# Attention scores as products of 64 rows, one head each, in the two halves of TensorE's rows

## The chip, the cores and the metric

The kernel runs on one core of a Trainium2 chip. The metric is device time in microseconds (us) of one execution. Before the change it is 565.6 us, the median of three runs (565.58 to 567.75). A profiled execution is somewhat longer, here 585.4 us; shares and single durations are read from it, the total is not.

In the notation of the profile, PE is TensorE's matmul row, PEld its weight loads, DVE is VectorE, ACT is ScalarE, POOL is GpSimd, and SP is SyncE, which issues most of the DMA transfers here. "L662" is line 662 of the kernel.

## The reference

Two blocks follow each other. The first is attention with a local window: 4 batches, 8 heads, 768 tokens, 64 elements a head. A chunk of 32 queries sees 8 memory keys and the keys from 16 before its start to 8 after its end. The second sends each token to the one of 8 experts with the highest gate, and scales the result by the gate.

```python
for c in range(nc):
    q_c = q[:, :, c_start:c_end]
    k_full = np.concatenate([mem_k, k[:, :, l_start:r_end]], axis=2)
    v_full = np.concatenate([mem_v, v[:, :, l_start:r_end]], axis=2)
    scores = scale * np.matmul(q_c, k_full.transpose(0, 1, 3, 2))
    a = softmax(scores)                      # written out in the reference
    out[:, :, c_start:c_end] = np.matmul(a, v_full)
x = out.transpose(0, 2, 1, 3).reshape(B * S, H * D)      # 3072 x 512
expert_idx = np.argmax(x @ w_gate, axis=1)
y[rows of e] = np.maximum(x[rows of e] @ w1[e], 0) @ w2[e]   # 512 -> 1024 -> 512
return gate_w[:, None] * y
```

## The kernel before

Everything is float32. The attention works on 32 blocks of 96 queries (QB = 96), and each block looks at a window of 128 keys. Queries and keys arrive by DMA for two blocks at a time, in token rows; TensorE transposes them, so that the 64 elements of a head lie on 64 partitions: even heads on partitions 0 to 63, odd heads on 64 to 127. Two heads thus share 128 partitions. The keys of such a pair stand as the weights of the array (128 rows by 128 keys). The queries stream through it, and each head's queries have zeros in the other head's half:

```python
qTs = [kpool.tile([128, H // 2, 2, 2, QB], F32, name=f"qT{i}") for i in range(NQ)]
for i, t in enumerate(qTs):
    nc.vector.memset(t[0:D, :, 1], 0.0)
    nc.gpsimd.memset(t[D:128, :, 0], 0.0)
...
def turn_heads(name, u, x):
    t = ps_t.tile([128, H // 2, QB], F32, tag="t", name="tqk")
    for a in range(H // 2):
        turn(t[:, a], units[u][name][:, 2 * a + x], ident[0:QB, 0:QB])
    return t

def turn_q(u, x):
    units[u]["qT"] = qTs[u % NQ]
    t = turn_heads("q", u, x)
    for j in range(2):
        (nc.vector.tensor_copy if x else nc.scalar.copy)(
            qTs[u % NQ][D * x : D * x + D, :, x, j], t[D * j : D * j + D]
        )
...
def scores(i):
    s, (b, qb) = st[i], divmod(i, NQB)
    w0 = window(qb)
    p0 = QB // 2 * (i % 2)
    sc = ps_s.tile([128, H, 128], F32, tag="s", name="sc")
    for a in range(H // 2):
        mm(
            sc[:, 2 * a : 2 * a + 2, 0:QB].rearrange("p x (j t) -> p x j t", j=2),
            lhsT=turned[b][:, a, w0 : w0 + WIN],
            rhs=units[i // 2]["qT"][:, a, :, :, p0 : p0 + QB // 2],
            start=True,
            stop=True,
        )
    ex = s["ex"] = apool.tile([128, H, QB], F32, name="ex")
    ...                                       # three exponentials over all heads, on ScalarE

def values(i, g, bank):
    ...
    for j in range(4):
        h = 4 * g + j
        mm(o[:, j], lhsT=s["ex"][:, h], rhs=s["v"][:, h], start=True, stop=True)
    ...                                       # VectorE divides by the sums and writes x
```

One turn of the attention's loop holds, in this order on TensorE, work of several blocks (cut; the rest of a turn is routing and DMA issues):

```python
for i in range(NB + 3):
    ...                                       # loads for later blocks
    if u < NU:
        f(u, 0)                               # half of the transposes of a later q or k
    need(i, scores)
    ...
    if 0 <= i - 1 < NB:
        values(i - 1, 0, banks[0])
    need(i - 2, turn_xb)                      # transposes of the result, for the gate
    late = logits(i - 3, banks[1]) if 0 <= i - 3 < NB else None
    if 0 <= i - 1 < NB:
        values(i - 1, 1, banks[1])
    ...
    if u < NU:
        f(u, 1)                               # the other half of the transposes
```

PSUM holds two `sc` tiles of two banks each, two tiles of transposes and two banks for `values` and `logits`. A block's keys window lies in `turned[b]`, with the memory keys between the keys of each block; they come there through four transposes of 32 rows at the start (`tm`, line 615). The experts follow the attention in the same program.

Of the kernel before, what the change touches and what calls it, by code (L numbers as in the profile page):

```python
# [10 lines left out]
F32 = mybir.dt.float32  # L11
# [8 lines left out]
B, H, S, D = 4, 8, 768, 64  # L20
NMEM = 8
CHUNK, LEFT, RIGHT = 32, 16, 8
QB = 96
# [41 lines left out]
WIN = 128  # L65
PER = QB + NMEM
KW = NQB * PER
NV, NQ = 6, 3
# [25 lines left out]
def window(qb):  # L94
    return min(max(PER * qb - LEFT, 0), KW - WIN)
# [415 lines left out]
def ordinary(ctx, tc, q, k, v, mem_k, mem_v, moe_w_gate, moe_w1, moe_w2, out, good):  # L511

    nc = tc.nc
    mm, turn = nc.tensor.matmul, nc.tensor.transpose

    def bc(ap, axis, n):
        shape = list(ap.shape)
        shape.insert(axis, n)
        idx = tuple([slice(None)] * axis + [None])
        return ap[idx].to_broadcast(shape)  # L520
# [6 lines left out]
    kpool = actx.enter_context(tc.tile_pool(name="kpool", bufs=1))  # L527
# [23 lines left out]
    wg = cpool.tile([128, DM // 128, E], F32, name="wg")  # L551
    nc.scalar.dma_start(wg, moe_w_gate.rearrange("(c p) e -> p c e", p=128))

    qTs = [kpool.tile([128, H // 2, 2, 2, QB], F32, name=f"qT{i}") for i in range(NQ)]
    for i, t in enumerate(qTs):
        nc.vector.memset(t[0:D, :, 1], 0.0)
        nc.gpsimd.memset(t[D:128, :, 0], 0.0)

    mk = kpool.tile([B * NMEM, H, D], F32, name="mk")
    for b in range(B):  # L560
# [35 lines left out]
    turned = {}  # L596

    units = [dict() for _ in range(NU)]
# [20 lines left out]
# [10 lines that stand above are left out]
        t = turn_heads("q", u, x)  # L629
        for j in range(2):  # L630
            (nc.vector.tensor_copy if x else nc.scalar.copy)(
                qTs[u % NQ][D * x : D * x + D, :, x, j], t[D * j : D * j + D]
            )

    def place_mem(b):
# [20 lines left out]
    def scores(i):  # L656
        s, (b, qb) = st[i], divmod(i, NQB)
        w0 = window(qb)
        p0 = QB // 2 * (i % 2)
        sc = ps_s.tile([128, H, 128], F32, tag="s", name="sc")  # L660
        for a in range(H // 2):
            mm(  # L662
                sc[:, 2 * a : 2 * a + 2, 0:QB].rearrange("p x (j t) -> p x j t", j=2),
                lhsT=turned[b][:, a, w0 : w0 + WIN],
                rhs=units[i // 2]["qT"][:, a, :, :, p0 : p0 + QB // 2],
                start=True,
                stop=True,
            )
        ex = s["ex"] = apool.tile([128, H, QB], F32, name="ex")
        x = 0 if qb == 0 else 2 if qb == NQB - 1 else 1  # L670
        sc4 = sc[:, :, 0:QB].rearrange("p h (j t) -> p h j t", j=2)
        ex4 = ex.rearrange("p h (j t) -> p h j t", j=2)
        for g in range(3):
            sl = slice(CHUNK // 2 * g, CHUNK // 2 * g + CHUNK // 2)
            nc.scalar.activation(  # L675
                ex4[:, :, :, sl], sc4[:, :, :, sl], AF.Exp, bias=mask[:, 3 * x + g : 3 * x + g + 1], scale=D**-0.5
            )

    def values(i, g, bank):
        s = st[i]  # L680
        if g == 0:
            s["x"] = xr[:, i % NXR, 0:DM]
        o = bank[0:QB, 0 : 4 * (D + 1)].rearrange("p (h d) -> p h d", h=4)
        for j in range(4):
            h = 4 * g + j
            mm(o[:, j], lhsT=s["ex"][:, h], rhs=s["v"][:, h], start=True, stop=True)  # L686

        inv = inv_all[:, i, 4 * g : 4 * g + 4]
        nc.vector.reciprocal(inv, o[:, :, D])  # L689
        x = s["x"].rearrange("p (h d) -> p h d", h=H)  # L690
        nc.vector.tensor_tensor(x[:, 4 * g : 4 * g + 4], o[:, :, 0:D], bc(inv, 2, D), op=OP.mult)
# [162 lines left out]
    with tc.manual_schedule():  # L854
# [8 lines left out]
        for name, u in ((turn_k, 0), (turn_q, 0), (turn_k, 1)):  # L863
            name(u, 0)
            name(u, 1)
            if name is turn_q:
                turn_mem()
                place_mem(0)
        for i in range(NB + 3):

            u = i // 2 + 1 + i % 2
            which, f = ("q", turn_q) if i % 2 == 0 else ("k", turn_k)
            if i % 2 == 0 and u + 2 < NU:
                load_unit("k", k, u + 2)
# [3 lines left out]
            if u < NU:  # L878
                f(u, 0)
            need(i, scores)  # L880
            banks = [ps_o.tile([128, 512], F32, tag="o", name="o") for _ in range(2)]
            then = []
# [5 lines left out]
            if 0 <= i - 1 < NB:  # L888
                values(i - 1, 0, banks[0])
# [3 lines left out]
            if 0 <= i - 1 < NB:  # L893
                values(i - 1, 1, banks[1])
# [16 lines left out]
            for g in range(last):  # L911
                t = GROUPS[g][0] + i - GROUPS[g][1] - 4
# [28 lines left out]
    h = mpool.tile([128, KH, 2, HALF], F32, name="h")  # L941
# [341 lines left out]
@with_exitstack  # L1283
def kernel(ctx, tc, *args):
    nc = tc.nc
    gpool = ctx.enter_context(tc.tile_pool(name="gpool", bufs=1))
    good = gpool.tile([1, 1], I32, name="good")
    rv = ordinary(tc, *args, good)
    with tc.If(rv == 0):
        general(tc, *args)  # L1290
# [28 lines left out]
```

## Time and profile before

| part of the span | us | what TensorE does there |
|---|---|---|
| 0 to 14.6 | 14.6 | waits for the first loads, first transposes |
| 14.6 to about 160 | 145.4 | the 32 blocks; matmul row busy 139.7 us, weight loads 137.7 us |
| 160 to 220 | 60.0 | routing, last scatters, a first short run of experts; matmul row busy 55.5 us |
| 220 to 570 | 350.0 | the experts; matmul row busy 334.0 us |

A matmul's duration in the profile runs from its start to its modelled end, and matmuls follow each other before that end. So durations add up to more than the time, and what one costs is the distance between starts. A float32 matmul shows as two records, each with a weight load; a float32 transpose shows as one. In the groups of part 5, the shape is weights (rows*columns) followed by the streamed columns, then the count, the busy time and the mean duration in ns, and last the idle time of the engine just before, with what ended it.

The profile's granted TensorE clock is 1.00 for most of the attention stage and 0.5 in its first microseconds.

### The profile page before, as it was taken

What the parts mean: (1) busy time and instruction counts of PE and PEld (TensorE: products, weight loads), DVE (VectorE), ACT (ScalarE), POOL (GpSimd) and SP (SyncE); (2) the same over time, 40 slices, a digit from 0 to 9 for tenths busy, and PEclk for the clock granted to TensorE, in tenths of its full rate; (3) what the DMA queues carried; (4) which work ended last, traced back from release to release, by engine and by line L of the source; (5) the groups of instructions that cost most, each with busy time, mean ns of one, the idle gap of its engine ahead of it and who ended that gap; (6) DMA issues with size and microseconds to landing.
All of it is one profiled execution on the core that took longest, in us unless ns stands there. A gap on an engine that the chain in (4) does not pass through costs nothing. (4 is left out here: it accounts for less than half of the span.)

```text
span 585.4 us, 10593 instructions
## 1 busy us (share of the span) xinstructions
PE 534.9 (91%) x3850; PEld 503.9 (86%) x3850; DVE 323.7 (55%) x757; ACT 175.8 (30%) x414; POOL 133.9 (23%) x174
## 2 busy tenths in 40 slices
PE   3999899999999899988999999979999999999950
PEld 3999899999978489988899999969999999988850
DVE  4556555656536519539378368356393874929220
ACT  3556455645412113023231132122232402232010
POOL 3500212313154630050240043230201503010020
PEclk9999999999959999988999999998999999999985
DMA  9999999999132256082252184230232807200010
GB/s 173 187 170 203 229 192 231 210 214 219 31 94 83 74 169 225 13 284 99 91 200 78 34 294 119 85 142 1 67 125 97 308 8 251 94 19 10 0 47 32
DMA packets 81655, 76.13 MB, mean 130 GB/s; under 512 B 39852, under 2 KB 64556, under 8 KB 81456
## 3 DMA queue, kind: packets, MB, share of 16 engines
q1 hardware_dynamic: 72368, 54.54, 39.8%
q0 software_dynamic: 8128, 19.29, 9.8%
q14 instruction: 147, 1.20, 0.7%
q8 instruction: 52, 0.85, 0.6%
q10 hardware_dynamic: 960, 0.24, 0.2%
HBM read 65.04 MB, written 16.45 MB: 139 GB/s over the span
## 5 line engine op out<-in xcount | busy, mean ns | idle before, releaser
L1023 POOL DMA_INDIRECT out_dram<-y,tg x36 | 39.0, 1084 | 135.3 <-ACT y L1017 115.6
L1113 ACT ACTIVATE h<-h 128x288 f32<-128x288 f32 (+6 forms) x72 | 33.7, 476 | 110.9 <-DVE h L1142 53.3
L1086 PE MATMUL b<-xT,w 128*128 128x256 f32 (+1 forms) x288 | 60.7, 369 | 0.0
L1086 PEld LDWEIGHTS b<-xT,w 128*128 128x128 f32 x288 | 52.3, 190 | 6.7 <-issue 0.5
L686 PE MATMUL o<-v,ex 128*96 128x65 f32 x512 | 55.6, 253 | 1.0 <-PE o L686 1.0
L686 PEld LDWEIGHTS o<-v,ex 128*96 128x96 f32 x512 | 52.2, 169 | 1.1 <-issue 1.1
L662 PE MATMUL sc<-qT,kT 128*128 128x192 f32 x256 | 50.4, 342 | 0.0
L675 ACT ACTIVATE ex<-sc,cst 128x256 f32<-128x256 f32 x96 | 38.4, 470 | 30.7 <-PE sc L662 27.4
L1086 PE MATMUL b<-h,w 128*128 128x144 f32 (+6 forms) x288 | 46.6, 317 | 0.0
L825 POOL DMA_INDIRECT xe<-x_dram,rows x38 | 40.8, 1074 | 25.0 <-PE b L1086 10.8
L1086 PE MATMUL b<-xS,w 128*128 128x144 f32 (+6 forms) x288 | 46.4, 311 | 0.0
L1086 PEld LDWEIGHTS b<-h,w 128*128 128x128 f32 x288 | 43.7, 201 | 0.8
L1086 PE MATMUL b<-xS,wT 128*128 128x144 f32 (+6 forms) x288 | 44.4, 307 | 0.0
L1086 PE MATMUL b<-big,w 128*128 128x144 f32 (+6 forms) x288 | 44.4, 307 | 0.0
L662 PEld LDWEIGHTS sc<-qT,kT 128*128 128x128 f32 x256 | 43.1, 199 | 0.0
L1086 PE MATMUL b<-big,wT 128*128 128x144 f32 (+6 forms) x288 | 42.9, 307 | 0.0
L1124 ACT COPY big<-b 128x288 f32<-128x288 f32 (+6 forms) x18 | 7.6, 425 | 117.2 <-PE b L1086 102.7
L1086 PEld LDWEIGHTS b<-xS,w 128*128 128x128 f32 x288 | 42.1, 194 | 0.8
L689 DVE RECIPROCAL inv_all<-o 96x4 f32<-96x4 f32 x64 | 11.4, 178 | 55.9 <-PE o L686 47.5
L1086 PEld LDWEIGHTS b<-xS,wT 128*128 128x128 f32 x288 | 41.2, 190 | 1.1 <-issue 0.3
L1086 PEld LDWEIGHTS b<-big,w 128*128 128x128 f32 x288 | 41.4, 190 | 0.8
L1086 PEld LDWEIGHTS b<-big,wT 128*128 128x128 f32 x288 | 41.0, 190 | 0.8
(150 smaller groups left out, 863.6 us busy)
## 6 DMA issues: line engine op xcount, KB each, us to landing
w<-in_moe_w_dram SPq DMA_DIRECT2D x64, 512.0 KB
kn<-in_k_dram SPq DMA_DIRECT2D x16, 384.0 KB
qn<-in_q_dram SPq DMA_DIRECT2D x16, 384.0 KB
v<-in_v_dram SPq DMA_DIRECT2D x24, 128.0 KB
v<-in_v_dram SPq DMA_DIRECT2D x24, 112.0 KB
v<-in_v_dram SPq DMA_DIRECT2D x8, 144.0 KB
v<-in_v_dram SPq DMA_DIRECT2D x8, 96.0 KB
xe<-x_dram,rows POOLq DMA_INDIRECT x38
```

The costliest lines, as they stand in the source:

```text
L662: mm(sc[:, 2 * a : 2 * a + 2, 0:QB].rearrange("p x (j t) -> p x j t", j=2), lhsT=turned[b][:, a, w0 : w0 + WIN], rhs=units[i // 2]["qT"][: ...
L675: nc.scalar.activation(ex4[:, :, :, sl], sc4[:, :, :, sl], AF.Exp, bias=mask[:, 3 * x + g : 3 * x + g + 1], scale=D**-0.5)
L686: mm(o[:, j], lhsT=s["ex"][:, h], rhs=s["v"][:, h], start=True, stop=True)
L689: nc.vector.reciprocal(inv, o[:, :, D])
L825: nc.gpsimd.indirect_dma_start(out=to.bitcast(I32), out_offset=None, in_=x_dram, in_offset=bass.IndirectOffsetOnAxis(ap=which, axis=0), bo ...
L1023: i = nc.gpsimd.indirect_dma_start(out=out, out_offset=bass.IndirectOffsetOnAxis(ap=token.bitcast(I32), axis=0), in_=y, in_offset=None, bo ...
L1086: mm(bank[:, q, 0:hf], lhsT=w[i][:, c, 128 * (q0 + q) : 128 * (q0 + q) + 128], rhs=a[i][:, c], start=c == 0, stop=c == k - 1,)
L1113: relu = lambda o: nc.scalar.activation(o, o, AF.Relu)
L1124: nc.scalar.copy(T(p), P(1, p))
```

## The change

Each head becomes a product of its own. Its weights are its keys alone (64 rows by 128 keys), and its 96 queries stream through these 64 rows. Even heads use rows 0 to 63 of the array and odd heads rows 64 to 127, and the code takes them in turn. The zero halves of the query tile are no longer needed, nor are the six memsets that wrote them. The scores of the even heads go to one bank of PSUM and those of the odd heads to the other, so the order of heads in `sc` and `ex` becomes even heads first, and `values` reads its weights from there. The aim is to stop streaming columns against zeros and to let the two row halves of the array work side by side.

```diff
--- before.py
+++ after.py
@@ -551,10 +551,7 @@
     wg = cpool.tile([128, DM // 128, E], F32, name="wg")
     nc.scalar.dma_start(wg, moe_w_gate.rearrange("(c p) e -> p c e", p=128))
 
-    qTs = [kpool.tile([128, H // 2, 2, 2, QB], F32, name=f"qT{i}") for i in range(NQ)]
-    for i, t in enumerate(qTs):
-        nc.vector.memset(t[0:D, :, 1], 0.0)
-        nc.gpsimd.memset(t[D:128, :, 0], 0.0)
+    qTs = [kpool.tile([128, H // 2, 2, QB], F32, name=f"qT{i}") for i in range(NQ)]
 
     mk = kpool.tile([B * NMEM, H, D], F32, name="mk")
     for b in range(B):
@@ -629,7 +626,7 @@
         t = turn_heads("q", u, x)
         for j in range(2):
             (nc.vector.tensor_copy if x else nc.scalar.copy)(
-                qTs[u % NQ][D * x : D * x + D, :, x, j], t[D * j : D * j + D]
+                qTs[u % NQ][D * x : D * x + D, :, j], t[D * j : D * j + D]
             )
 
     def place_mem(b):
@@ -657,15 +654,18 @@
         s, (b, qb) = st[i], divmod(i, NQB)
         w0 = window(qb)
         p0 = QB // 2 * (i % 2)
+
         sc = ps_s.tile([128, H, 128], F32, tag="s", name="sc")
         for a in range(H // 2):
-            mm(
-                sc[:, 2 * a : 2 * a + 2, 0:QB].rearrange("p x (j t) -> p x j t", j=2),
-                lhsT=turned[b][:, a, w0 : w0 + WIN],
-                rhs=units[i // 2]["qT"][:, a, :, :, p0 : p0 + QB // 2],
-                start=True,
-                stop=True,
-            )
+            for x in range(2):
+                half = slice(D * x, D * x + D)
+                mm(
+                    sc[:, H // 2 * x + a, 0:QB].rearrange("p (j t) -> p j t", j=2),
+                    lhsT=turned[b][half, a, w0 : w0 + WIN],
+                    rhs=units[i // 2]["qT"][half, a, :, p0 : p0 + QB // 2],
+                    start=True,
+                    stop=True,
+                )
         ex = s["ex"] = apool.tile([128, H, QB], F32, name="ex")
         x = 0 if qb == 0 else 2 if qb == NQB - 1 else 1
         sc4 = sc[:, :, 0:QB].rearrange("p h (j t) -> p h j t", j=2)
@@ -683,7 +683,7 @@
         o = bank[0:QB, 0 : 4 * (D + 1)].rearrange("p (h d) -> p h d", h=4)
         for j in range(4):
             h = 4 * g + j
-            mm(o[:, j], lhsT=s["ex"][:, h], rhs=s["v"][:, h], start=True, stop=True)
+            mm(o[:, j], lhsT=s["ex"][:, H // 2 * (h % 2) + h // 2], rhs=s["v"][:, h], start=True, stop=True)
 
         inv = inv_all[:, i, 4 * g : 4 * g + 4]
         nc.vector.reciprocal(inv, o[:, :, D])
```

## The prediction

> **What bounds the kernel now.** I read the page first, then the order of matmuls in one block of the attention stage, then the waits of the queue that issues the loads. The first two lines of the page's part 1 show TensorE's two rows busy nearly all the time; the three groups of part 5 are the line that changes and one that feeds from it.
>
> ```profile
> PE 534.9 (91%) x3850; PEld 503.9 (86%) x3850; DVE 323.7 (55%) x757; ACT 175.8 (30%) x414; POOL 133.9 (23%) x174
> ...
> L662 PE MATMUL sc<-qT,kT 128*128 128x192 f32 x256 | 50.4, 342 | 0.0
> L675 ACT ACTIVATE ex<-sc,cst 128x256 f32<-128x256 f32 x96 | 38.4, 470 | 30.7 <-PE sc L662 27.4
> ...
> L662 PEld LDWEIGHTS sc<-qT,kT 128*128 128x128 f32 x256 | 43.1, 199 | 0.0
> ```
>
> The scores are 32 blocks x 4 matmuls = 128 instructions, but 256 records: each float32 product is a weight load and a matmul, twice. Neither row was idle before them (0.0), while ScalarE waited 27.4 us for them. The durations 342 and 199 ns overlap, so what a product costs has to be read from the start times. One block of the steady part, from the timeline of TensorE alone (start, duration, line, count):
>
> ```profile
> 29.68 1.49 PE L662 MATMUL sc<-qT,kT 128*128 128x192 f32 x8
> 31.01 0.81 PE L686 MATMUL o<-v,ex 128*96 128x65 f32 x8
> 31.66 0.50 PE L696 MATMUL tx<-cst,big 96*128 96x96 f32 x4
> 32.00 0.77 PE L710 MATMUL o<-wg,xT 128*96 128x8 f32 x8
> 32.62 0.87 PE L686 MATMUL o<-v,ex 128*96 128x65 f32 x8
> 33.33 0.50 PE L623 MATMUL tqk<-cst,qn 96*128 96x96 f32 x4
> 33.67 0.49 PE L623 MATMUL tqk<-cst,kn 96*128 96x96 f32 x4
> 34.00 1.49 PE L662 MATMUL sc<-qT,kT 128*128 128x192 f32 x8
> ```
>
> From 29.68 to 34.00 is 4.32 us a block without a hole, so the stage is bound by TensorE. The scores hold it from 29.68 to 31.01: 1.33 us for 8 records, 166 ns each. All their time is on the path; 32 blocks make 42.6 us, the most that could be won here.
>
> Is it the stream or the weight load that sets 166 ns? Four more groups of the timeline, from the experts, give the rule:
>
> ```profile
> 506.85 1.95 PE L1086 MATMUL b<-big,w 128*128 128x96 f32 x16
> 508.63 1.95 PE L1086 MATMUL b<-h,w 128*128 128x96 f32 x16
> ...
> 239.63 2.12 PE L1086 MATMUL b<-big,w 128*128 128x144 f32 x16
> 241.59 3.62 PE L1086 MATMUL b<-xT,w 128*128 128x256 f32 x16
> ```
>
> 144 columns: (241.59 - 239.63) / 16 = 122 ns. 256 columns: the last of the 16 starts about 3.24 us after the first (3.62 less the 0.379 us of one record), so 216 ns. That is 0.84 ns a column and a constant of about 2 ns: the stream sets it, and 192 columns make 163 ns, as the scores show. But 96 columns should then take 82 ns and take (508.63 - 506.85) / 16 = 111 ns. So a new set of 128 weight columns has a floor of about 112 ns. The changed products have 96 columns each and lie on that floor.
>
> [...] The kernel has one place that bears on the last: four transposes of 32 rows between transposes of 96 rows, at the half clock of the start. No trace of it bears on the overlap. [...]
>
> ```profile
> 11.12 0.60 PE L615 MATMUL tm<-cst,mk 32*128 32x32 f32 x4 [1.51 <-DMA mk<-in_mem_k_dram]
> 11.65 0.90 PE L623 MATMUL tqk<-cst,kn 96*128 96x96 f32 x4
> ```
>
> One record of the first kind lasts 0.289 us, so the last of the four starts at 11.72 - 0.289 = 11.43; the next kind starts at 11.65, 0.22 us later, where its fellows follow at 0.10. Its own second record is late too: a record lasts 0.37 us there, so the fourth starts at 11.65 + 0.90 - 0.37 = 12.18, so three gaps take 0.53 instead of 3 x 0.16 = 0.48. Together about 0.17 us for one switch, at half clock. If the part in the array halves at full clock and the part of the weight load doesn't, a switch costs 0.08 to 0.17 us. This is an estimate from one place.
>
> **The change part by part.**
> 1. Six memsets of the zero halves go: three of 0.70 us on VectorE, three of 0.73 us on GpSimd, all over by 3.5 us, while the first transpose waits for its data until 5.82. Worth 0.
> 2. The copies that fill qT keep their size (64x384, 474 and 556 ns), the exponentials theirs (128x256, 470 ns). The order of heads is only a matter of addresses. Worth 0.
> 3. Four products of 192 columns (8 records) become eight of 96 (16 records), in pairs over the two row halves. Half of the columns that streamed before met zeros, so the columns per head halve; the weight loads double in number, each of 64 rows by 128 columns.
>    - If loads and streams of the two halves run side by side, each half has 8 records at 112 ns: 8 x 112 = 0.90 us against 1.33, a gain of 0.43 us a block.
>    - If the loads go one after another: 16 x 112 = 1.79 us, a loss of 0.46 us a block.
> 4. Before and after the scores stand products of 96 and 128 rows. So there are two switches a block, 0.17 to 0.33 us together.
>
> The sum with side-by-side loads: 0.90 + 0.25 = 1.15 against 1.33, 0.18 us a block, 5.8 us over 32 blocks (3.2 to 8.3 with the span of the switches). One after another: 1.79 + 0.25 - 1.33 = 0.71 us, 23 us more.
>
> **Does the gain reach the end?** The loads might not follow. In 14.6 to 144 us the DMA engines show a share of over 1 and 187 to 217 GB/s, so I read what the issuing queue waits for there:
>
> ```profile
> SPq L603 <- PE tqk L623: 7.0, 9, 2.4
> SPq L603 <- PE sc L662: 4.1, 3, 2.3
> SPq L603 <- PE o L686: 2.6, 4, 1.9
> SPq L603 <- PE tx L696: 2.5, 2, 2.1
> SPq L610 <- PE o L686: 1.9, 1, 1.9
> ```
>
> It waits 18 us of 129 for TensorE to release buffers, about 14%. A block shorter by 0.2 us (5%), even by 0.43 (10%), is still fed. VectorE and ScalarE are busy for 85 and 80 of the 145 us of the stage. Behind the attention the experts begin when the last block is counted and sent, so a shorter stage moves them forward whole.
>
> **The rivals.** (a) Loads serialize: for it, the weight floor of 111 ns shows the load path is already a limit, and each product is two passes of the same row half in sequence, not alternating halves. [...] It gives 565.6 + 23 = 588. (b) Everything overlaps and switches are nearly free: 32 x 0.43 = 13.8 us less, 552. Against it, the 0.17 us seen after the transposes of 32 rows. (c) The loads by DMA become the bound: the time stays within 3 us of before. Its share of over 1 speaks for it, the 14% of waits against it. (d) The switches cost more than estimated[...]: 0.45 us a block would eat the gain and leave 566.
>
> **Range and chances.** I give the side-by-side loads 0.6, less certain because two passes stand in each half. With them the time lies between 552 and 566, most likely at 565.6 - 5 = 561; 2% is 11.3 us, so only rival (b) or nearly that is faster by over 2%: a third of the 0.6. Without them (0.4) it is mostly 580 to 591, beyond 2%, unless loads overlap in part. So 0.20 faster, 0.47 within 2%, 0.33 slower; the range 552 to 590 has to hold both branches, and the middle between them is the least likely.
>
> **What would show it.** In the changed profile: 512 records on the line of the scores, and the time from the first of them to the next group per block, near 1.15 us (loads overlap), 0.9 (switches free) or over 1.9 (loads serial). Start times of pairs a few ns apart would show the overlap; a hole between the last transpose and the first score the switch. The other groups of the block should keep their lengths, and new waits of the transposes for kn or qn would be the DMA. I am wrong if the time leaves 552 to 590, or if the block is shorter but the attention stage ends no earlier.

## The result and the profile after

The changed kernel takes 671.1 us, the median of four runs (669.75 to 672.66), against 565.8 us for the kernel before (four runs, 565.58 to 567.75). The ratio is 1.185, with a 95% interval of 1.182 to 1.189. That is 105 us more, far outside the predicted range of 552 to 590. Ratios, here and below, leave out runs over 1.5% above the fastest of their kernel.

The page of the profile after, part 1 and the granted clock of part 2 (40 slices, tenths), and from part 5 the values (line 686), the scores (line 662) and the exponentials (line 675):

```profile
PE 631.6 (95%) x4106; PEld 591.1 (88%) x4106; DVE 321.8 (48%) x754; ACT 178.4 (27%) x414; POOL 131.3 (20%) x171
...
PEclk9999999999999999999999999999999999999995
...
L686 PE MATMUL o<-v,ex 128*96 128x65 f32 x512 | 97.5, 369 | 0.9 <-PE o L686 0.9
L686 PEld LDWEIGHTS o<-v,ex 128*96 128x96 f32 x512 | 88.2, 278 | 5.5 <-issue 4.2
...
L662 PE MATMUL sc<-qT,kT 64*128 64x96 f32 x512 | 64.8, 431 | 0.0
L675 ACT ACTIVATE ex<-sc,cst 128x256 f32<-128x256 f32 x96 | 38.5, 471 | 71.1 <-PE sc L662 71.0
```

TensorE is busier than before, not waiting more. But the values of line 686, whose size and number the change leaves alone (only the head that they read from `ex` is found elsewhere), went from a mean of 253 ns to 369. ScalarE's exponential is where it was, 471 ns against 470. One block in the timeline of TensorE (start, duration, what) shows it better:

```profile
38.53 2.02 PE L662 MATMUL sc<-qT,kT 64*128 64x96 f32 x16
40.48 1.54 PE L686 MATMUL o<-v,ex 128*96 128x65 f32 x8
41.82 0.84 PE L696 MATMUL tx<-cst,big 96*128 96x96 f32 x4
42.46 1.34 PE L710 MATMUL o<-wg,xT 128*96 128x8 f32 x8
43.65 1.52 PE L686 MATMUL o<-v,ex 128*96 128x65 f32 x8
44.97 0.84 PE L620 MATMUL tqk<-cst,qn 96*128 96x96 f32 x4
45.61 0.84 PE L620 MATMUL tqk<-cst,kn 96*128 96x96 f32 x4
46.38 2.03 PE L662 MATMUL sc<-qT,kT 64*128 64x96 f32 x16
```

From 38.53 to 46.38 a block takes 7.85 us against 4.32 before. Every group but the scores has about doubled: line 710 from 0.62 us (32.00 to 32.62) to 1.19, the two groups of transposes from 0.67 us to 1.41, with their switch (the change between products over different numbers of rows). Only the scores grew less, from 1.33 to 1.95 us. By these start distances TensorE runs at half clock through the whole attention, and its matmul row is busy for all of it (237.4 of the 237.4 us from 14.6 to 252.0). The first and the last scores start at 14.7 and 252.0 us, 237.3 us apart; before they were 142.2 us apart. Before's profiled run was itself 20 us longer than its timed runs, so it is a poor measure here. Against the control with fillers below (135.1 us), the attention lost 102 us, which is the whole 105 but for 3.

The clock row of the page says 9 in these slices. It can't be believed: the trace's own clock records begin with their first change, which is the opening at 274.3 us, and the row fills the time ahead of it with full clock. The start distances agree with the record and not with the row: equal products of the experts follow each other at 427 ns up to 273.97 us and at 216 ns from 274.36 us on. The same filling hid the half clock of the first 17.5 us before, where transposes follow each other at 160 ns (12.02 to 12.82 us) and only from 17.54 us on at 83: the profile shows 1.00 there, so my sentence on the clock ahead of the prediction, that it grants 0.5 in the first microseconds, is wrong as a reading of the profile. The half clock follows from the start times alone. That sentence also leaves out that before's clock closed for 3.4 us at 72.1 us, inside the attention, with 0.5 in its record. The distance between starts is the evidence: 0.16 us a transpose in (0.84 - 0.36) / 3, against 0.08 in the fast kernel.

The pairs do run side by side. Four single records of the scores, start in us and row half by the order of the code:

```
38.529  even head, first pass
38.536  odd head
38.851  even head
38.857  odd head
```

The two of a pair start 6 to 7 ns apart. The second pair comes 0.32 us after the first; the six behind it follow at 213 ns each, nearly twice the 112 ns that I had given them.

### The profile page after: what moved, and what is told of

It reads as the page before. It is cut to its first block, busy times and chain, and to the rows that moved or that the text cites. A ratio compares the mean times of both kernels' runs of the same rounds, so it can differ in the third digit from the quotient of the medians.

```text
span 668.0 us, 11099 instructions
## 1 busy us (share of the span) xinstructions
PE 631.6 (95%) x4106; PEld 591.1 (88%) x4106; DVE 321.8 (48%) x754; ACT 178.4 (27%) x414; POOL 131.3 (20%) x171
## 5 line engine op out<-in xcount | busy, mean ns | idle before, releaser
L686 PE MATMUL o<-v,ex 128*96 128x65 f32 x512 | 97.5, 369 | 0.9 <-PE o L686 0.9
L686 PEld LDWEIGHTS o<-v,ex 128*96 128x96 f32 x512 | 88.2, 278 | 5.5 <-issue 4.2
L662 PE MATMUL sc<-qT,kT 64*128 64x96 f32 x512 | 64.8, 431 | 0.0
L662 PEld LDWEIGHTS sc<-qT,kT 64*128 64x128 f32 x512 | 57.1, 324 | 7.0 <-issue 6.7
L710 PEld LDWEIGHTS o<-wg,xT 128*96 128x96 f32 x256 | 44.7, 280 | 0.0
L1086 PE MATMUL b<-h,w 128*128 128x144 f32 (+6 forms) x288 | 44.3, 307 | 0.0
L710 PE MATMUL o<-wg,xT 128*96 128x8 f32 x256 | 42.7, 297 | 0.0
L773 POOL DMA_INDIRECT x_dram<-big,dest x32 | 29.7, 927 | 64.0 <-DVE dest L765 38.2
L1086 PEld LDWEIGHTS b<-h,w 128*128 128x128 f32 x288 | 41.3, 190 | 0.8
```

The lines of the kernel that those rows point to most:

```text
L662: mm(sc[:, H // 2 * x + a, 0:QB].rearrange("p (j t) -> p j t", j=2), lhsT=turned[b][half, a, w0 : w0 + WIN], rhs=units[i // 2]["qT"][half, ...
L686: mm(o[:, j], lhsT=s["ex"][:, H // 2 * (h % 2) + h // 2], rhs=s["v"][:, h], start=True, stop=True)
L710: mm(ps, lhsT=s["xT"][:, c], rhs=wg[:, c], start=c == 0, stop=c == DM // 128 - 1)
L773: i = nc.gpsimd.indirect_dma_start(out=x_dram, out_offset=bass.IndirectOffsetOnAxis(ap=dest[:, t : t + 1], axis=0), in_=xr[:, t % NXR].bit ...
L1086: mm(bank[:, q, 0:hf], lhsT=w[i][:, c, 128 * (q0 + q) : 128 * (q0 + q) + 128], rhs=a[i][:, c], start=c == 0, stop=c == k - 1,)
```

## The experiments

Theory A, a guess of mine: with half the columns streamed, the attention is too sparse for the clock to open, and nothing before the experts opens it. Rivals: A2, it is the 64-row products or their switches, not the missing columns; B, the clock is only lost at the start, and once open it stays; C, something other than the clock slows TensorE.

Each of the first four kernels ran once, on one chip, where the kernel before took 567.1 us.

**The burst at the start.** Eight full matmuls ahead of the loop, in the changed kernel:

```diff
+        warm = ps_s.tile([128, H, 128], F32, tag="s", name="sc")
+        for _ in range(8):
+            mm(warm[:, 0:4], lhsT=ones, rhs=bc(ones, 1, 4), start=True, stop=True)
         for i in range(NB + 3):
```

> The changed kernel with eight matmuls of 128 rows by 512 columns ahead of the first block (16 records, about 10 us of added work), so that TensorE enters the attention at full clock. Theory A, the changed block is too sparse to keep the clock: [...] starts of paired scores are 213 ns apart again and the time is about 671 + 8 = 679 us. Theory B, only the warm start was lost and a warm TensorE stays warm: [...] a block of about 4.15 us, and a time near 561 + 8 = 569 us.

Measured: 571.2 us. A block deep in the attention, from the timeline of TensorE:

```profile
101.71 1.14 PE L662 MATMUL sc<-qT,kT 64*128 64x96 f32 x16
102.78 0.89 PE L686 MATMUL o<-v,ex 128*96 128x65 f32 x8
103.51 0.50 PE L696 MATMUL tx<-cst,big 96*128 96x96 f32 x4
...
105.94 1.14 PE L662 MATMUL sc<-qT,kT 64*128 64x96 f32 x16
```

A block takes 105.94 - 101.71 = 4.23 us, so the same code runs at full clock 80 us after the burst. The burst itself took 9 us (13.18 to 22.20). Without its cost that is about 562, where I had put the 64-row products at 561. Theory B holds in this run; C is out, since nothing but a burst at the start was added.

**The same sparse stream without 64 rows.** In the kernel before, the odd heads' scores are left out; their values use the even heads' exponentials. The output is thus not the reference's, and the experts get other tokens:

```diff
-                sc[:, 2 * a : 2 * a + 2, 0:QB].rearrange("p x (j t) -> p x j t", j=2),
+                sc[:, 2 * a, 0:QB].rearrange("p (j t) -> p j t", j=2),
                 lhsT=turned[b][:, a, w0 : w0 + WIN],
-                rhs=units[i // 2]["qT"][:, a, :, :, p0 : p0 + QB // 2],
+                rhs=units[i // 2]["qT"][:, a, 0, :, p0 : p0 + QB // 2],
...                                            # exponentials of the even heads only
-            mm(o[:, j], lhsT=s["ex"][:, h], rhs=s["v"][:, h], start=True, stop=True)
+            mm(o[:, j], lhsT=s["ex"][:, h - h % 2], rhs=s["v"][:, h], start=True, stop=True)
```

> The kernel before with the odd heads' scores left out (its odd heads use the even heads' exponentials): 4 products of 128 rows and 96 columns a block, so as few streamed columns in time as the changed kernel, but no 64-row products and no switches. Theory A1, the clock follows the share of time in which columns stream: half clock from the start, a block of about 7.6 us, attention ending near 250 us. Theory A2, [...] full clock, a block of about 3.9 us, attention ending near 150 us. The experts get other tokens here, so the attention stage is compared, not the whole.

Measured: 576.4 us, though it computes half the scores. Its scores in the timeline:

```profile
51.54 1.91 PE L662 MATMUL sc<-qT,kT 128*128 128x96 f32 x8
58.90 1.91 PE L662 MATMUL sc<-qT,kT 128*128 128x96 f32 x8
63.78 1.06 PE L662 MATMUL sc<-qT,kT 128*128 128x96 f32 x8
67.67 1.06 PE L662 MATMUL sc<-qT,kT 128*128 128x96 f32 x8
```

Blocks take 7.36 us until about 61 us and mostly 3.9 to 4.8 us after it, so neither forecast came true. Full rows without a switch also start at half clock and stay there for 46 us, where the kernel before opens its clock 3 us after its first scores: without the odd heads' columns the clock stays down that long, with 128 rows too. They are not the whole difference: here the clock opened in the attention after all, while the changed kernel's trace has it closed to the experts and its other three times are within 3 us of that run's.

**The 64-row products with more columns.** Six of eight products stream each head's queries twice; the second copy is overwritten by the next head, so the output stays the reference's:

```diff
-                    sc[:, H // 2 * x + a, 0:QB].rearrange("p (j t) -> p j t", j=2),
+                    sc[:, h0 : h0 + n, 0:QB].rearrange("p n (j t) -> p n j t", j=2),
                     lhsT=turned[b][half, a, w0 : w0 + WIN],
-                    rhs=units[i // 2]["qT"][half, a, :, p0 : p0 + QB // 2],
+                    rhs=bc(units[i // 2]["qT"][half, a, :, p0 : p0 + QB // 2], 1, n),
```

with `n = 2 if a + 1 < H // 2 else 1` and `h0 = H // 2 * x + a`.

> The changed kernel with 192 columns in six of the eight 64-row products of a block (each head's queries twice; the second copy is overwritten by the next head). Theory A1 (share of streaming): full clock, pairs 163 ns apart, a block of about 4.6 us and a time near 575 us. Theory A2 (64-row products count less, or the switches matter): half clock, pairs about 320 ns apart, a block of about 8.6 us and a time near 695 us.

Measured: 573.3 us, 98 us less than the changed kernel, with three quarters more columns in the scores:

```profile
18.79 2.66 PE L664 MATMUL sc<-qT,kT 64*128 64x192 f32 x16
24.07 1.44 PE L664 MATMUL sc<-qT,kT 64*128 64x192 f32 x16
28.07 1.44 PE L664 MATMUL sc<-qT,kT 64*128 64x192 f32 x16
```

The clock opens at 22.5 us, after two blocks. So 64-row products and switches don't keep it shut by themselves, which takes A2 in its plain form out.

**The old products, cut in two.** Eight products of 128 rows and 96 columns with the zeros, so all columns are kept and the loads doubled:

```diff
+            for x in range(2):
-                sc[:, 2 * a : 2 * a + 2, 0:QB].rearrange("p x (j t) -> p x j t", j=2),
+                sc[:, 2 * a + x, 0:QB].rearrange("p (j t) -> p j t", j=2),
-                rhs=units[i // 2]["qT"][:, a, :, :, p0 : p0 + QB // 2],
+                rhs=units[i // 2]["qT"][:, a, x, :, p0 : p0 + QB // 2],
```

> The kernel before with each 192-column product cut into two of 96 columns over all 128 rows, zeros kept: 16 records a block as in the changed kernel, same streamed columns as before, no 64 rows, no switches. With the weight floor of 112 ns the scores take 1.79 us and a block 4.8 us. Theory A1: streaming share falls only from 73 to 66% of a block, so likely full clock and about 580 us; if half clock, a block of 9.3 us and about 720 us. Theory A2: full clock, 580 us.

Measured: 578.3 us, the clock open from 20.0 us and blocks of 4.78 us. It also measures the floor of the weight load: 16 records take 1.79 us (102.13 - 100.34), 112 ns each.

```profile
100.34 1.95 PE L663 MATMUL sc<-qT,kT 128*128 128x96 f32 x16
102.13 0.82 PE L687 MATMUL o<-v,ex 128*96 128x65 f32 x8
```

**A quarter of the extra columns.** As the wide products, with `n = 2 if a == 0 else 1`, on a later chip where the kernel before took 565.1 us.

> The changed kernel with 192 columns in only two of the eight products of a block (the first even and the first odd head), no burst. It brackets the share of streaming that opens the clock: with six wide products it opened at 22.5 us, with none never. If the clock opens here after a few blocks: blocks of about 8.1 us, then of 4.35 us, and 570 to 600 us. If it stays closed: about 680 us.

Measured: 678.3 us; the clock stays closed to 281.9 us, in the experts. At half clock the products of 192 columns in the kernel before follow each other at 0.32 us (15.31 to 16.91 us), so 96 columns should stream for 0.16. The columns of the scores then make, for each block, with the two halves counted once where they run together:

| kernel | streaming of the scores, us at half clock | clock opens at, us |
|---|---|---|
| before | 8 x 0.32 = 2.56 | 17.5 |
| old products cut in two | 16 x 0.16 = 2.56 | 20.0 |
| 64 rows, six wide | 6 x 0.32 + 2 x 0.16 = 2.24 | 22.5 |
| 64 rows, two wide | 2 x 0.32 + 6 x 0.16 = 1.60 | 281.9 |
| half the heads, full rows | 8 x 0.16 = 1.28 | 61.0 |
| the changed kernel | 8 x 0.16 = 1.28 | 274.3 |

These are estimates from that distance, and each kernel has one trace. With 64 rows, 1.60 us a block did not open the clock in the attention and 2.24 us did. The fifth row breaks the order: at full rows less opened it. Whether 64 rows weigh less, or the more closely packed block only happened to meet the right moment, was not settled.

**The burst midway.** The same eight matmuls, but ahead of block 12 alone (`if i == 12:` before the scores).

> The changed kernel with the burst of eight full matmuls ahead of block 12 and none at the start. If a closed clock stays closed and an open one stays open on the same code: blocks of 7.85 us up to the burst at about 103 us, of 4.23 us after it, and 671 - 20 x 3.62 + 9 = about 608 us. If the start is what matters (loads, first blocks) and not the clock's own state: no change of pace at the burst and about 680 us.

Measured: 611.9 us, beside 565.1 for the kernel before.

```profile
86.07 2.03 PE L662 MATMUL sc<-qT,kT 64*128 64x96 f32 x16
94.56 2.03 PE L662 MATMUL sc<-qT,kT 64*128 64x96 f32 x16
102.28 9.13 PE L883 MATMUL sc<-ones 128*128 128x512 f32 x16
111.34 1.14 PE L662 MATMUL sc<-qT,kT 64*128 64x96 f32 x16
115.56 1.14 PE L662 MATMUL sc<-qT,kT 64*128 64x96 f32 x16
119.79 1.14 PE L662 MATMUL sc<-qT,kT 64*128 64x96 f32 x16
```

In one execution, the same blocks take 7.9 to 8.5 us ahead of the burst and 4.22 behind it. In this run the code left the clock as it found it, closed up to 102 us and open from 111 us on.

**The halves one after the other.** With the burst at the start, all even heads first:

```diff
-        for a in range(H // 2):
-            for x in range(2):
+        for x in range(2):
+            for a in range(H // 2):
```

> The changed kernel with the burst, but all even heads of a block first and then all odd heads, so that only one pair of neighbours lies in different row halves. If the two halves run side by side only when neighbours differ: 16 records at about 112 ns, scores 1.8 us instead of 1.07, a block of about 5.0 us and about 595 us. If the pairing of the order does not matter: 571 us as with the burst. If the streaming gets too thin and the clock falls: above 671 us.

Measured: 581.6 us. A block takes 4.74 us (104.94 - 100.20), the scores 1.58 us instead of 1.07. So the alternation in the code is worth 0.5 us a block, between the two forecasts (1.8 us without any overlap, 1.07 with all of it).

```profile
100.20 1.66 PE L662 MATMUL sc<-qT,kT 64*128 64x96 f32 x16
101.78 0.89 PE L686 MATMUL o<-v,ex 128*96 128x65 f32 x8
```

The single records do not name their half. Read by their distances, they are two rows of eight that each settle at 112 ns, and the second row starts with three records of the first still to come. If the second row is the odd heads, part overlaps in spite of the order.

**Can the gain be kept?** Nine fillers of 128 rows by 512 columns in the gaps of the start, where TensorE waits for loads anyway (in the changed kernel 5.45 us for the first keys, 1.70 for the memory keys and 0.86 for queries), were put into both kernels, and the wide products into the first three blocks alone. All three on one chip, beside the kernel before at 566.8 us (564.31 to 568.86, 11 runs).

```diff
+        keep_warm(4)                               # n matmuls as in the burst
         for name, u in ((turn_k, 0), (turn_q, 0), (turn_k, 1)):
             name(u, 0)
             name(u, 1)
+            keep_warm(1)
             if name is turn_q:
                 turn_mem()
                 place_mem(0)
+                keep_warm(1)
+        keep_warm(1)
```

> The changed kernel with nine filler matmuls of 128 rows by 512 columns in the idle gaps of the start (four while the first loads are under way, one after each of the early groups of transposes, two ahead of the loop). If a warm TensorE stays warm through the attention: a block of 4.23 us as in the run with the burst, no cost of the burst, and 560 to 564 us. If the gaps of the start close the clock again before the first block: half clock to the experts and about 671 us.

> The control: the same nine fillers in the kernel before. It gets the full clock some 10 us earlier than it did, which may be worth 1 to 4 us: 562 to 565 us. If the 64-row products themselves win at full clock (0.09 us a block, 3 us in all), this kernel is about 3 us slower than the changed kernel with the same fillers; if the gain there came from the earlier clock alone, both are equal.

> The changed kernel with 192 columns in the 64-row products of the first three blocks only. If the first blocks need only open the clock, it stays open with the narrow products after them: a block of 4.23 us and 563 to 567 us. If the narrow products can't hold it: the time falls back to 660 to 675 us.

| kernel | runs, us | median |
|---|---|---|
| 64 rows, fillers | 563.89 to 609.63 (6) | 592.9 |
| before, fillers | 563.67 to 567.0 (6) | 564.8 |
| 64 rows, three wide blocks | 564.84 to 587.78 (4) | 577.5 |

The control is 0.3% faster than the kernel before (ratio 0.997, 0.9945 to 0.9999). The changed kernel comes down to the same 564 in its best run, which is the one traced, with the clock open to 153.8 us, and is otherwise 14 to 46 us longer. The five longer runs have a lower mean clock over the whole run, 0.892 to 0.943 against 0.974, while all six of the control lie between 0.969 and 0.977; the longer the run, the lower its clock. Three wide blocks open the clock as well: the best of these four runs has it open from 19.4 to 156.0 us, and the other three are 12 to 23 us longer. So neither edit keeps the clock open in most runs, and neither beats the control.

In the best run with fillers the first and last scores are 133.0 us apart against 135.1 in the control, so the products win 2.1 us. The changed kernel, then the control, at the last group of values but one and at the first product of a short early run of the experts:

```profile
152.64 0.86 PE L686 MATMUL o<-v,ex 128*96 128x65 f32 x8 [0.95 <-PE o L686]
162.96 5.94 PE L1257 MATMUL b<-xT,w 128*128 128x256 f32 x16 [0.78 <-ACT xT L1016]
```

```profile
154.38 0.86 PE L686 MATMUL o<-v,ex 128*96 128x65 f32 x8 [0.95 <-PE o L686]
163.64 5.41 PE L1257 MATMUL b<-xT,w 128*128 128x256 f32 x16 [0.78 <-ACT xT L1016]
```

The lead is 1.7 us, then 0.7, and 0.1 at the first product of the experts' main run (198.3 against 198.4): the clock records show it closed for 13.7 us behind the attention against 10.2, and open again at 167 us in both. On these two traces the gain is gone there.

**What closes it again.** The fillers once more, to catch a long run:

> The changed kernel with the nine fillers once more, to catch in a trace what made five of its six timed runs 14 to 46 us longer than the profiled one (577.7 to 609.6 against 563.9). If the clock falls at a hole and the narrow products can't bring it back: one or more stretches of blocks of 7.85 us between blocks of 4.23 us, 3.6 us lost for each such block, and a time that fits (start at 564, so 4 to 13 slow blocks). If something else varies (the loads, the experts): all blocks of 4.23 us and the loss elsewhere.

Measured: 590.0 us. The scores, and what TensorE waited for between 117 and 126 us:

```profile
117.61 1.14 PE L662 MATMUL sc<-qT,kT 64*128 64x96 f32 x16
123.49 1.14 PE L662 MATMUL sc<-qT,kT 64*128 64x96 f32 x16
131.32 2.02 PE L662 MATMUL sc<-qT,kT 64*128 64x96 f32 x16
140.25 2.02 PE L662 MATMUL sc<-qT,kT 64*128 64x96 f32 x16
```

```profile
PE tqk L620 <- DMA kn<-in_k_dram: 1.4, 1, 1.4
PE o L686 <- DMA v<-in_v_dram: 0.8, 1, 0.8
```

Blocks of 4.2 to 5.9 us up to 123.49, then of 7.8 and 8.9. A load of k came 1.4 us late and one of v 0.8, the clock closed at 125.4 us and stayed so to 193.6. I took late loads for the cause of all such falls and moved the first expert's weights (eight transfers of 512 KB) behind the attention's loads, in both kernels:

```diff
-            if i % 3 == 0 and 6 <= i < 30:
-                fetch_w(0, (i // 3 - 2) // 4, (i // 3 - 2) % 4)
+            if i == NB - 2:
+                for n in range(8):
+                    fetch_w(0, n // 4, n % 4)
```

> The changed kernel with the nine fillers, and the first expert's weights (eight transfers of 512 KB, until now spread over the attention) issued only in turn 30 of the loop, behind the last loads of the attention. If late loads make the holes at which the clock falls: with some 20% less to load there are none, all six runs lie within 3 us of each other and at 560 to 566 us, unless the experts wait for the weights. If the holes have another cause: again a spread of 15 us and more between runs, up to 610 us.

> The control: the kernel before with the same nine fillers and the same late weights. Its clock never stayed down, so it stays steady and near 565 us. If the 64-row products are worth their 0.09 us a block once the clock holds, it is 2 to 3 us slower than the changed kernel with the same two edits; if the gain is lost behind the attention, equal.

Measured on one chip, where even the kernel before takes 583.1 us (578.51 to 587.27, 27 runs): the 64 rows 644.1 us (640.99 to 684.09, 6 runs; ratio to before 1.104, 1.099 to 1.109), the control 582.5 (22 runs; 1.000, 0.998 to 1.003). That fells late loads as the cause of all such falls. The two traces lie side by side; first the 64 rows:

```profile
64.54 1.14 PE L662 MATMUL sc<-qT,kT 64*128 64x96 f32 x16
72.69 2.03 PE L662 MATMUL sc<-qT,kT 64*128 64x96 f32 x16
80.55 2.03 PE L662 MATMUL sc<-qT,kT 64*128 64x96 f32 x16
88.40 2.03 PE L662 MATMUL sc<-qT,kT 64*128 64x96 f32 x16
```

and the control:

```profile
65.50 1.49 PE L662 MATMUL sc<-qT,kT 128*128 128x192 f32 x8
73.48 2.82 PE L662 MATMUL sc<-qT,kT 128*128 128x192 f32 x8
79.38 1.49 PE L662 MATMUL sc<-qT,kT 128*128 128x192 f32 x8
83.70 1.49 PE L662 MATMUL sc<-qT,kT 128*128 128x192 f32 x8
```

Both clocks fall at the same hole, in the turn that begins a new batch's keys: TensorE waits 0.9 and 1.0 us for ScalarE's copies into `kT` there, not for a load. The control, with its dense scores, is back in 6.8 us (69.9 to 76.7). The 64 rows stay closed from 67.7 to 238.4 us. The kernel before shows a fall in the same turn in its own profile, at 72.1 us, 3 us after a wait of 1.7 us for the same copies, and is back 3.4 us later. Why this chip is slower for every kernel, and why ScalarE's copies are late in that turn, stays open.

## Why the prediction was wrong

**The step that failed** is the sentence that the other groups of the block keep their lengths, and with it the use of full-clock durations throughout. In its place the runs showed every other group about doubled and a block of 7.85 us, where my sum gave 4.14; with a burst ahead the same code takes 4.23. I counted the columns against zeros as pure waste. They were a dense stream: where it was kept, the clock opened at 17.5 to 20.0 us, and again 3.4 and 6.8 us after the two holes above; where it was thinned and nothing else was added, the clock opened at 61.0 us or not before the experts. Six products with more columns over 64 rows opened it at 22.5. I had the half clock of the start before me, and a slice with a 5 in the clock row, and asked of neither what ended it. No rival of mine touched the clock.

**Loads and streams side by side**: right, though a guess: no trace ahead of the result showed it. The starts of a pair follow those of the last at 112 ns at full clock (with the burst) and at 213 at half (the changed kernel). That half the rows make the load no cheaper was assumed too, and the runs show it: the floor is 112 ns with 128 rows (the old products cut in two) and 112 with 64 within one half (the halves one after the other).

**Switches**: they cost time, as I had it; the size is just over the top of the range. At full clock the block shrank by 4.32 - 4.23 = 0.09 us, where I had 0.18. So scores and switches cost 1.33 - 0.09 = 1.24 us, and with 0.90 for the eight pairs the two switches take 0.34, against 0.17 to 0.33 estimated and 0.25 used. The single records of the burst run show the same time at the two edges of the scores: 0.09 us more than usual before the first pair and 0.07 behind it, 0.10 behind the last pair and 0.07 in the distance after. The old products cut in two, which have no switch, have none of these. Of the 5.8 us for 32 blocks this leaves 2.9; the run with fillers showed 2.1.

**The memsets and copies**: worth nothing, as said.

**The loads follow**: irrelevant at half clock, where the issuing queue waited 75.2 us for TensorE's transposes between 14.6 and 144 us. At full clock I was too sure: one trace has a load of k 1.4 us late.

**The gain reaches the end**: not in the pair of traces that can be compared; a longer closed clock behind the attention, 13.7 us against 10.2, took it.

**How long the clock stays closed.** The clock records of the kernel before hold five closures that begin and end within the run, each granting 0.5: four of 3.41 us (at 72.1, 259.9, 266.7 and 396.4 us) and one of 17.07 (at 160.9), five times as long. The closures above that were timed in other runs, 6.8, 10.2, 13.7, 68.2 and 170.7 us, lie near multiples of 3.41 as well; why was not shown. A busy matmul row alone did not open the clock: the changed kernel had it 100% busy through the attention, at half clock. I had timed weight loads and streams and did not ask what the change would do to the clock.

## What to carry to other kernels

Before taking work from TensorE, ask whether that work is what keeps its clock open: compare the starts of equal matmuls before and after (transposes at 83 against 160 ns here), and read the clock from those distances. Here a sparse stage held both states, so one good run or a burst at the start proves little. After a hole of about 1 us the kernel with dense scores had its clock back in 6.8 us, the sparse one not in 170. Here the zeros were worth their columns.

## What was unexpected of the hardware

- The same blocks ran at 7.85 or 4.23 us with nothing but their past to tell them apart, and held either state through the attention: the first and the last scores start 132.1 us apart with the burst (22.6 to 154.7 us) and 237.3 without.
- Of the profile and not the chip: the clock row of the page shows full clock for all time ahead of the first recorded change, 274.3 us here.
- Weight loads slow down with the clock. Products of 96 streamed columns on 128 weight columns follow each other at 112 ns with the burst and, within a half, at 213 in the changed kernel; those of 8 or 65 on 96 weight columns (logits of line 710, values of line 686) at 85 ns in the kernel before and at 160 in the changed one, whichever of the two they stream.
- With the halves one after the other in the code, the 16 records read as two rows of eight, 112 ns apart in each, the second starting ahead of the first's last three. So the order between the halves seems not to have been kept; the records do not name the half, and no run settled it.
